# Value rows of even and of odd chunks both whole from DRAM

## The chip, the cores and the metric

The kernel runs on one core of a Trainium2 chip. Five engines work side by side, each through its own list of instructions in order: TensorE (PE, with its weight loads PEld), VectorE (DVE), ScalarE (ACT), GpSimd (POOL) and SyncE (SP). SyncE computes nothing here; it issues every transfer between DRAM and the core's SBUF (128 partitions), and 16 DMA engines carry them out. The metric is the device time of one execution in microseconds (us).

## What is computed

Chunked local attention, then a soft mixture of experts, all in float32. The attention has 4 batches x 8 heads, 768 positions, head size 64. The positions are cut into chunks of 32; each chunk attends to 8 memory rows, the 16 positions before it, its own 32 and the 8 after it, 64 keys in all:

```python
for c in range(nc):
    l_start, r_end = max(0, c_start - 16), min(S, c_end + 8)
    k_full = np.concatenate([mem_k, k[:, :, l_start:r_end]], axis=2)
    v_full = np.concatenate([mem_v, v[:, :, l_start:r_end]], axis=2)
    a = softmax(scale * q_c @ k_full^T)
    out[:, :, c_start:c_end] = a @ v_full
```

Its output x (3072 tokens x 512) goes through the experts: logits x @ phi (32 slots); a softmax over all tokens gives each slot's input; 8 experts with two layers (512 to 1024 to 512, ReLU) work on 4 slots each; a softmax over the slots mixes their outputs back to every token. The expert weights w1 and w2 are 16.8 MB each.

## The kernel before, in words

The attention runs over 12 units of 256 positions (8 chunks, 8 heads). A unit's queries `q_t`, keys `k_t` and values `v_t` lie in one of three buffers each (`NB`), heads in pairs: on the partitions of `k_t` and `v_t` rows of the first and of the second head of a pair alternate, and each has its own half of the free axis, with zeros where the other head's rows are. Those zeros are written once, ahead of the loop; that is why every load of keys or values goes to every second partition, once for each head (`load_k`, `load_v`).

Two neighbouring chunks, an even and an odd one, share 32 of their 64 key rows. Before the change `v_t[i]` is a pair of tiles. The even one takes all 64 rows from the DRAM tensor `vw`, on partitions 0 to 127 in steps of two, 256 KB a head. The odd one takes the 32 rows that it does not share from `vx`, on partitions 0 to 63 in steps of two, 128 KB a head; its partitions 64 to 127 are the even tile's, copied by GpSimd (`share_v`, L150).

The loop over units (L407) interleaves: values of unit i and their normalizing, scores and softmax of unit i + 2, transposes of unit i + 1, and, every second unit, the logits of a group of two units. In each pass SyncE gets, in program order, the values of unit i + 3 (once unit i has used the buffer), weight pieces of 512 KB by a table (`load_w`, 1.5 pieces a pass at first), and keys and queries of unit i + 5. GpSimd gets the key copies `first_k(i + 3)` and `share_v(i + 2)`. After the loop the weights fill what buffers come free, including those of keys, queries, values and x; the experts follow, and `combine` writes the output.

Transfers are carried out in the order of their issue, with at most eight on the way: each has one of eight semaphores, and the ninth waits for the first.

Each engine keeps the order in which the program is written (`InOrder`), so the opening (L188 to L217) fixes what stands behind what: the clears of `k_t` and `v_t` on DVE, ACT and POOL, the loads of units 0 to 2, and the copies of GpSimd between them.

In the row names a tile's buffer number is left out, and a helper records every operation, so that all of them carry the line L65.

Of the kernel before, what the change touches and what calls it, by code (L numbers as in the profile page):

```python
# [10 lines left out]
F32 = mybir.dt.float32  # L11
# [4 lines left out]
P = 128  # L16
B, H, S, D = 4, 8, 768, 64
# [17 lines left out]
NSLOT = 32  # L35
# [35 lines left out]
def tile_attn_softmoe(  # L71
# [2 lines left out]
    qT: bass.AP,  # L74
    kT: list,
    vw: bass.AP,
    vx: bass.AP,
    phi: bass.AP,
    w1: bass.AP,
    w2: bass.AP,  # L80
# [7 lines left out]

    q_t = [cp.tile([P, NPAIR, U], F32, tag=f"q{i}", name=f"q{i}") for i in range(NB)]
    k_t = [cp.tile([P, 2, KW], F32, tag=f"k{i}", name=f"k{i}") for i in range(NB)]  # L90
    v_t = [[cp.tile([P, 2, VW], F32, tag=f"v{i}{o}", name=f"v{i}{o}") for o in range(2)] for i in range(NB)]
    x_t = [cp.tile([P, 4, DM], F32, tag=f"x{i}", name=f"x{i}") for i in range(2)]
    w_slab = [cp.tile([P, PIECE], F32, tag=f"w{i}", name=f"w{i}") for i in range(NW)]
    lT = cp.tile([P, NG, P], F32, tag="lT", name="lT")
    late = [v_t[(NU - NB) % NB][o].rearrange("p a n -> p (a n)") for o in range(2)]
    hT = late[0].rearrange("p (e f s) -> p e f s", e=E, s=NSLOT)
    c_sb = late[1][:, 0:4 * NG * NSLOT].rearrange("p (u s) -> p u s", s=NSLOT)
    cst = [late[1][:, 4 * NG * NSLOT + P * G:4 * NG * NSLOT + P * G + P] for G in range(NG)]
# [16 lines left out]
    def load_q(u):  # L115
        sp.dma_start(q_t[u % NB], qT[u])
# [10 lines left out]
    def load_k(u):  # L127
        for h in range(2):
            sp.dma_start(own_k(u)[h:P:2, h], kT[u % UPB][u // UPB, 64 * h:64 * h + 64])
# [11 lines left out]
        pool.tensor_copy(out=kx[:, :, :, lo:CHUNK], in_=own[:, :, :, 0:CHUNK - lo])  # L141

    def load_v(u):
        e, o = v_t[u % NB]
        for h in range(2):
            sp.dma_start(e[h:P:2, h], vw[u, 64 * h:64 * h + 64])
        for h in range(2):
            sp.dma_start(o[h:P // 2:2, h], vx[u, CHUNK * h:CHUNK * h + CHUNK])

    def share_v(u):  # L150
        e, o = v_t[u % NB]
        pool.tensor_copy(out=o[P // 2:P], in_=e[P // 2:P])

    slabs = list(w_slab)
    freed = []
    for d in range(NB):
        u = NU - NB + d
        flat = k_t[u % NB].rearrange("p a n -> p (a n)")
        freed += [(2 * u - 3, flat[:, 0:PIECE]), (2 * u - 3, flat[:, PIECE:2 * PIECE])]
        freed += [(2 * u - 3, q_t[u % NB].rearrange("p g n -> p (g n)"))]  # L160
        if d:
            freed += [(2 * u, v_t[u % NB][o][:, a]) for o in range(2) for a in range(2)]
    flat_x = [t.rearrange("p u n -> p (u n)") for t in x_t]
    last = (NG - 1) % 2
    freed += [(2 * NU, flat_x[1 - last][:, 0:PIECE]), (2 * NU, flat_x[1 - last][:, PIECE:2 * PIECE])]
# [19 lines left out]

    dve.memset(k_t[0][:, 0], 0.0)  # L188
    dve.memset(warm, 0.0)
    pool.memset(k_t[0][:, 1], 0.0)  # L190
    make_identity(nc, ident)
    load_q(0)
    load_k(0)
    dve.memset(v_t[0][1][0:P // 2], 0.0)
    dve.memset(k_t[1][:, 0], 0.0)
    pool.memset(k_t[1][:, 1], 0.0)
    for u in range(NB):
        e = v_t[u][0].rearrange("p h n -> p (h n)")
        act.copy(out=e, in_=warm[:, 0:1].broadcast_to([P, 2 * VW]))
    load_k(1)  # L200
    load_q(1)
    load_v(0)
    first_k(0)
    dve.memset(v_t[1][1][0:P // 2], 0.0)
    share_v(0)
    load_v(1)
    sp.dma_start(phi_sb, phi.rearrange("(kc p) s -> p kc s", p=P))
    first_k(1)
    dve.memset(k_t[2][:, 0], 0.0)
    pool.memset(k_t[2][:, 1], 0.0)  # L210
    load_k(2)
    load_q(2)
    share_v(1)
    pool.memset(v_t[2][1][0:P // 2], 0.0)
    load_v(2)
    first_k(2)
    load_w(W0)  # L217
# [42 lines left out]
    def softmax(u, tiles):  # L260
        mx = wk.tile([P, 16, 1], F32, tag="mx", name=f"mx{u}")
        p = pexp[u] = wk.tile([P, 8, 4 * CHUNK], F32, tag="p", name=f"p{u}")
        step = NSUB // len(tiles)
        for a, t in enumerate(tiles):
            if u % UPB == 0 and a == 0:
                dve.memset(t[0:32, 0, :, :, 0:LEFT], NEG)
            if u % UPB == UPB - 1 and a == len(tiles) - 1:
                dve.memset(t[96:128, step - 1, :, :, CHUNK - RIGHT:CHUNK], NEG)
            m = mx[:, 8 * step * a:8 * step * (a + 1)]
            dve.tensor_reduce(out=m[:, :, 0], in_=t.rearrange("p s g h n -> p (s g h) n"), axis=AX.X, op=ALU.max)  # L270
            for h in range(2):
                dve.tensor_tensor(
                    out=p[:, 4 * step * a:4 * step * (a + 1)].rearrange("p m (n h) -> p h m n", h=2)[:, h],
                    in0=t.rearrange("p s g h n -> p h (s g) n")[:, h],
                    in1=m.rearrange("p (m h) o -> p h m o", h=2)[:, h].broadcast_to([P, 4 * step, 2 * CHUNK]),
                    op=ALU.subtract,
                )

# [25 lines left out]
    def values(u, pt):  # L304
        a_ps = banks(f"a{u}", "A").rearrange("p s (g h d) -> p s g h d", g=NPAIR, h=2)
        for s in range(NSUB):
            for g in range(NPAIR):
                for j in range(4):
                    v = v_t[u % NB][j % 2].rearrange("p h (i g d) -> p h i g d", g=NPAIR, d=D)
                    pe.matmul(  # L310
                        a_ps[32 * j:32 * j + 32, s, g],
                        lhsT=pt[s][:, g, 32 * j:32 * j + 32],
                        rhs=v[:, :, 2 * s + j // 2, g, :],
                        start=True, stop=True,
                    )
        return a_ps
# [90 lines left out]
    for i in range(NU):  # L407
        G = (i - 2) // 2 if i >= 2 else None
        first = i % 2 == 0
        if i >= 1:  # L410
            transpose_x(i - 1)
        if i + 1 < NU:
            exponent(i + 1)
        if G is not None and not first:
            dispatch_t(G)
        a_ps = values(i, pt)
        if G is not None and first:
            l_ps = logits(G)
        if G is not None and not first:
            dispatch(G)  # L420
        normalize(i, a_ps)
        if i + 3 < NU:
            load_v(i + 3)
        load_w(W0 + int(WRATE * (i + 0.5)) if i < WLAST else usable[2 * i])
        if G is not None and first:
            dispatch_max(G, l_ps)
            dispatch_exp(G, l_ps)
        if G is not None and not first:
            dispatch_z(G)
            dispatch_sum(G)  # L430
        if i + 2 < NU:
            softmax(i + 2, scores(i + 2))
        if i + 1 < NU:
            pt = transpose_p(i + 1)
            normalizer(i + 1)
        if i + 3 < NU:
            first_k(i + 3)
        if i + 2 < NU:
            share_v(i + 2)
        if i + 5 < NU:  # L440
            load_k(i + 5)
            load_q(i + 5)
        load_w(W0 + int(WRATE * (i + 1)) if i < WLAST else usable[2 * i + 1])
        if i == NU - NB + 1:
            pool.memset(hT, 0.0)
# [169 lines left out]
def _layouts(inputs):  # L615
    q, k, v = inputs["q"], inputs["k"], inputs["v"]
    qT = q.reshape(B, NPAIR, 2, UPB, U, D).transpose(0, 3, 5, 2, 1, 4).reshape(NU, P, NPAIR, U)

    def stream(x, mem):
        half = CHUNK // 2  # L620
        parts = [np.zeros((B, H, LEFT, D), x.dtype), x[:, :, :half]]
        for t in range(half, S, 2 * CHUNK):
            parts += [mem, x[:, :, t:t + 2 * CHUNK]]
        parts.append(np.zeros((B, H, RIGHT, D), x.dtype))
        return np.concatenate(parts, axis=2)

    ks = stream(k, inputs["mem_k"]).reshape(B, NPAIR, 2, STREAM, D)
    kT = {}
    for u in range(UPB):
        base = CP * STEP * u  # L630
        chain = [base + STEP * i + r for i in range(CP) for r in list(range(CHUNK)) + list(range(2 * CHUNK, STEP))]
        chain += [base + STEP * CP + r for r in range(HALO)]
        chain = chain[LEFT if u == 0 else HALO:len(chain) - (RIGHT if u == UPB - 1 else 0)]
        both = [base + STEP * i + CHUNK + r for i in range(CP) for r in range(CHUNK)]
        cols = ks[:, :, :, np.array(chain + both)]
        kT[f"k{u}"] = cols.transpose(0, 2, 4, 1, 3).reshape(B, P, NPAIR * NCOL[u])

    vs = stream(v, inputs["mem_v"]).reshape(B, NPAIR, 2, STREAM, D)

    def windows(first):  # L640
        rows = np.array([[[STEP * (CP * u + i) + r for i in range(CP)] for u in range(UPB)] for r in first])
        w = vs[:, :, :, rows]
        return w.transpose(0, 4, 2, 3, 5, 1, 6).reshape(NU, 2 * len(first), CP, NPAIR * D)

    vw = windows(range(2 * CHUNK))
    vx = windows(range(2 * CHUNK, STEP + HALO))
    w2 = inputs["moe_w2"].reshape(E, NFC, P, NBLK, WB).transpose(3, 0, 2, 1, 4).reshape(NBLK, E, P, 2, PIECE)
    return {"qT": qT, **kT, "vw": vw, "vx": vx, "phi": inputs["moe_phi"], "w1": inputs["moe_w1"], "w2": w2}


# [17 lines left out]
```

## Time and profile before

| | |
|---|---|
| runs | 193.74, 190.03, 191.42 us; median 191.42 |
| the profiled execution | 187.95 us, span 186.2 us |
| PE busy | 146.5 us (79%) |
| DVE busy | 101.2 us (54%) |
| ACT busy | 62.7 us (34%) |
| POOL busy | 36.3 us (19%), 22.7 of it copies of values |
| DMA | 63.12 MB, mean 339 GB/s, queue of SyncE 95.2% of 16 engines' span |

Busy time is the time in which an engine ran an instruction; shares are of the span, from the first instruction to the last. The profiled execution's own time is 1.75 us longer than its span, and below the three runs. The DMA share is the mean over 16 DMA engines of the time in which a packet was on the way, so a share of 1.00 says that the engines had work, not that they moved it fast: that is in GB/s.

### The profile page before, as it was taken

The page shows a single profiled execution, that of the slowest core. Times are in us where ns is not written, and L with a number is a line of the kernel's source. Part 1 is how long each engine was busy: PE and PEld are TensorE (multiplying, and loading weights), DVE is VectorE, ACT ScalarE, POOL GpSimd, SP SyncE. Part 2 cuts the span into 40 slices and gives each one's busy share as a digit, 9 for nine tenths or more (in the row PEclk, how much of TensorE's full clock was granted, in tenths as well). Part 3 has the DMA queues.
Part 4 walks back from the last instruction along what each step waited for, and adds up shares of the span by engine and source line. Part 5 has one row for each costly group of instructions (what it writes and reads, how often), then busy time and mean ns, then how long its engine had stood idle before and what let it go on. Part 6 is the DMA issues. An engine that isn't in the chain of part 4 may idle for free.

```text
span 186.2 us, 6128 instructions
## 1 busy us (share of the span) xinstructions
PE 146.5 (79%) x2649; PEld 108.2 (58%) x2649; DVE 101.2 (54%) x179; ACT 62.7 (34%) x122; POOL 36.3 (19%) x43
## 2 busy tenths in 40 slices
PE   4821996884999599789799588579999978867960
PEld 4711795773879488659778485264565635411530
DVE  6860399592679959597899934320560007100360
ACT  7620136231624806354273362200322006000350
POOL 6006901452223404050521800000000000000000
PEclk9996699999699999999999969957999999975576
DMA  5699789999999999999999999999999999999596
GB/s 164 217 276 219 229 258 383 340 392 284 386 293 314 323 338 383 260 362 258 334 303 263 388 402 415 410 407 408 408 410 406 409 406 408 408 411 420 213 407 249
DMA packets 18219, 63.12 MB, mean 339 GB/s; under 512 B 3088, under 2 KB 3088, under 8 KB 18192
## 3 DMA queue, kind: packets, MB, share of 16 engines
q1 hardware_dynamic: 18192, 62.73, 95.2%
q8 instruction: 21, 0.34, 0.8%
q14 instruction: 6, 0.05, 0.1%
HBM read 56.43 MB, written 6.29 MB: 337 GB/s over the span
## 4 chain that ended last, share of the span: by engine, by line
PE 46%; DMA 20%; DVE 16%; issue 7%; ACT 5%; SPq 1%; DVEq 0%; POOL 0%; ACTq 0%
PE s L65 10%; PE a L65 8%; PE h L65 7%; DMA w<-in_w_dram 5%; DMA k<-in_w_dram 5%; DMA v<-in_w_dram 5%; PE xt_ps L65 5%; PE pt_ps L65 4%; DMA v<-in_vw_dram 4%; DVE p L65 4%; DVE z L65 3%; DVE mx L65 3%; PE o L65 3%; ACT v L65 3%; DVE x L65 3%
## 5 line engine op out<-in xcount | busy, mean ns | idle before, releaser
L65 PE MATMUL s<-k,q 128*32 128x128 f32 x768 | 27.5, 292 | 13.9 <-POOL k L65 8.1
L65 PEld LDWEIGHTS s<-k,q 128*32 128x32 f32 x768 | 23.9, 118 | 18.3 <-issue 8.9
L65 POOL COPY v<-v 64x2048 f32<-64x2048 f32 x12 | 22.7, 1896 | 52.0 <-DMA v<-in_vw_dram 37.0
L65 PE MATMUL a<-v,pt 128*32 128x128 f32 x768 | 25.1, 277 | 4.6 <-issue 4.4
L65 ACT COPY pt<-pt_ps 128x512 f32<-128x512 f32 x24 | 13.1, 590 | 40.3 <-PE pt_ps L65 40.1
L65 PEld LDWEIGHTS a<-v,pt 128*32 128x32 f32 x768 | 20.8, 111 | 8.1 <-issue 6.4
L65 DVE TENSOR_REDUCE mx<-s 128x16 f32<-128x1024 f32 (+1 forms) x13 | 14.8, 1142 | 14.0 <-PE s L65 13.7
L65 DVE TENSOR_TENSOR x<-a,z 128x1024 f32<-128x1024 f32 x12 | 14.7, 1224 | 8.1 <-PE a L65 7.2
L65 PE MATMUL pt_ps<-ident,p 128*128 128x128 f32 x96 | 14.6, 298 | 2.5 <-issue 2.3
L65 DVE TENSOR_TENSOR p<-s,mx 128x512 f32<-128x512 f32 (+1 forms) x26 | 15.8, 656 | 0.5
L65 ACT ACTIVATE p<-p 128x1024 f32<-128x1024 f32 (+1 forms) x13 | 12.9, 994 | 7.0 <-DVE p L65 6.7
L65 PE MATMUL xt_ps<-ident,x 128*128 128x128 f32 x96 | 14.5, 298 | 0.9 <-DVE x L65 0.5
L65 ACT COPY xT<-xt_ps 128x512 f32<-128x512 f32 x24 | 13.4, 604 | 4.7 <-PE xt_ps L65 4.7
L65 DVE TENSOR_REDUCE z<-p 128x16 f32<-128x1024 f32 x12 | 14.6, 1214 | 0.0
L65 PEld LDWEIGHTS pt_ps<-ident,p 128*128 128x128 f32 x96 | 11.3, 150 | 5.2 <-issue 4.6
L65 PEld LDWEIGHTS xt_ps<-ident,x 128*128 128x128 f32 x96 | 12.4, 155 | 2.0 <-DVE x L65 1.4
L65 DVE COPY so_sb<-so 128x256 f32<-128x256 f32 x2 | 0.8, 424 | 19.7 <-PE so L65 19.7
L65 PE MATMUL o<-shl,v 32*128 32x256 f32 x96 | 9.8, 530 | 1.4 <-ACT shl L65 0.9
L65 PEld LDWEIGHTS o<-shl,v 32*128 32x128 f32 x96 | 6.5, 249 | 5.0 <-ACT shl L65 2.0
L65 POOL COPY k<-k 128x192 f32<-128x192 f32 (+2 forms) x20 | 5.8, 295 | 17.9 <-DMA k<-in_k_dram 17.2
L65 ACT COPY shl<-r 128x256 f32<-128x256 f32 x2 | 0.7, 373 | 23.5 <-PE r L65 23.5
L65 PE MATMUL h<-w,siT 128*32 128x256 f32 x120 | 8.5, 443 | 0.0
(95 smaller groups left out, 169.9 us busy)
## 6 DMA issues: line engine op xcount, KB each, us to landing
w<-in_w_dram SPq DMA_DIRECT2D x30, 512.0 KB, 9.8
q<-in_qT_dram SPq DMA_DIRECT2D x12, 512.0 KB, 7.2
v<-in_vw_dram SPq DMA_DIRECT2D x24, 256.0 KB, 7.9
k<-in_w_dram SPq DMA_DIRECT2D x12, 512.0 KB, 10.1
v<-in_w_dram SPq DMA_DIRECT2D x12, 512.0 KB, 10.2
v<-in_vx_dram SPq DMA_DIRECT2D x24, 128.0 KB, 7.6
q<-in_w_dram SPq DMA_DIRECT2D x6, 512.0 KB, 10.1
k<-in_k_dram SPq DMA_DIRECT2D x8, 296.0 KB, 7.0
```

What stands on the lines that cost most here:

```text
L65: return self.tc.keep_in_program_order(f(*args, **kwargs))
```

## The change

`v_t[i]` becomes one tile with an axis for even and odd. For each head, one transfer of 512 KB brings both whole: 64 partitions in steps of two, and on each two pieces of 4 KB. `vx` and `share_v` go. To let even and odd chunks use one layout, the rows of a window are ordered so that its two halves alternate (`even`, `odd` in `_layouts`), and the subtraction of the maximum (in `softmax`) writes the scores in that order: it reads PSUM with an innermost axis of two elements, 32 elements apart. phi is laid out by the host so that each partition reads one row of 512 bytes. The opening is written in another order: all four clears of value buffers 0 and 1 on ScalarE, those of buffer 2 on VectorE and GpSimd, the clears of all three key buffers first on VectorE and ahead of the first key copy on GpSimd.

```diff
-    v_t = [[cp.tile([P, 2, VW], F32, tag=f"v{i}{o}", name=f"v{i}{o}") for o in range(2)] for i in range(NB)]
+    v_t = [cp.tile([P, 2, 2, VW], F32, tag=f"v{i}", name=f"v{i}") for i in range(NB)]
...
     def load_v(u):
-        e, o = v_t[u % NB]
+
         for h in range(2):
-            sp.dma_start(e[h:P:2, h], vw[u, 64 * h:64 * h + 64])
-        for h in range(2):
-            sp.dma_start(o[h:P // 2:2, h], vx[u, CHUNK * h:CHUNK * h + CHUNK])
-
-    def share_v(u):
-        e, o = v_t[u % NB]
-        pool.tensor_copy(out=o[P // 2:P], in_=e[P // 2:P])
+            sp.dma_start(v_t[u % NB][h:P:2, :, h], vw[u, 64 * h:64 * h + 64])
...
+    def clear_v(eng, u, o):
+        t = v_t[u][:, o].rearrange("p h n -> p (h n)")
+        if eng is act:
+            act.copy(out=t, in_=warm[:, 0:1].broadcast_to([P, 2 * VW]))
+        else:
+            eng.memset(t, 0.0)
+
+    dve.memset(warm, 0.0)
     dve.memset(k_t[0][:, 0], 0.0)
-    dve.memset(warm, 0.0)
     pool.memset(k_t[0][:, 1], 0.0)
+    for u in range(2):
+        clear_v(act, u, 0)
+        clear_v(act, u, 1)
     make_identity(nc, ident)
+    dve.memset(k_t[1][:, 0], 0.0)
+    pool.memset(k_t[1][:, 1], 0.0)
     load_q(0)
     load_k(0)
-    dve.memset(v_t[0][1][0:P // 2], 0.0)
-    dve.memset(k_t[1][:, 0], 0.0)
-    pool.memset(k_t[1][:, 1], 0.0)
-    for u in range(NB):
-        e = v_t[u][0].rearrange("p h n -> p (h n)")
-        act.copy(out=e, in_=warm[:, 0:1].broadcast_to([P, 2 * VW]))
     load_k(1)
     load_q(1)
-    load_v(0)
-    first_k(0)
-    dve.memset(v_t[1][1][0:P // 2], 0.0)
-    share_v(0)
-    load_v(1)
-    sp.dma_start(phi_sb, phi.rearrange("(kc p) s -> p kc s", p=P))
-    first_k(1)
     dve.memset(k_t[2][:, 0], 0.0)
     pool.memset(k_t[2][:, 1], 0.0)
+    clear_v(dve, 2, 0)
+    first_k(0)
+    load_v(0)
+    load_v(1)
+    sp.dma_start(phi_sb, phi)
+    first_k(1)
+    clear_v(pool, 2, 1)
     load_k(2)
     load_q(2)
-    share_v(1)
-    pool.memset(v_t[2][1][0:P // 2], 0.0)
     load_v(2)
     first_k(2)
...
                 dve.tensor_tensor(
-                    out=p[:, 4 * step * a:4 * step * (a + 1)].rearrange("p m (n h) -> p h m n", h=2)[:, h],
-                    in0=t.rearrange("p s g h n -> p h (s g) n")[:, h],
-                    in1=m.rearrange("p (m h) o -> p h m o", h=2)[:, h].broadcast_to([P, 4 * step, 2 * CHUNK]),
+                    out=p[:, 4 * step * a:4 * step * (a + 1)].rearrange("p m (j s h) -> p h m j s", s=2, h=2)[:, h],
+                    in0=t.rearrange("p s g h (b j) -> p h (s g) j b", b=2)[:, h],
+                    in1=m.rearrange("p (m h) o -> p h m o", h=2)[:, h].rearrange(
+                        "p m (o z) -> p m o z", z=1).broadcast_to([P, 4 * step, CHUNK, 2]),
                     op=ALU.subtract,
                 )
...
-        if i + 2 < NU:
-            share_v(i + 2)
...
-    vw = windows(range(2 * CHUNK))
-    vx = windows(range(2 * CHUNK, STEP + HALO))
+    even = [CHUNK * (r % 2) + r // 2 for r in range(2 * CHUNK)]
+    odd = [CHUNK * (2 - r % 2) + r // 2 for r in range(2 * CHUNK)]
+    vw = np.stack([windows(even), windows(odd)], axis=2)
+    phi = inputs["moe_phi"].reshape(NKC, P, NSLOT).transpose(1, 0, 2)
```

How instructions move, at two places. First GpSimd in the opening; `k_67`, `k_68` and `k_69` are the key buffers 0, 1 and 2, `v_70` and `v_71` the even and odd value tile of buffer 0, `v_72` and `v_73` those of buffer 1. Before:

```order
L65 MEMSET k_68 128x1312
L65 COPY k_67<-k_67 128x2x4x16
L65 COPY v_71<-v_70 64x2048
L65 COPY k_68<-k_67 128x2x4x24
L65 COPY k_68<-k_68 128x2x4x8
L65 MEMSET k_69 128x1312
L65 COPY v_73<-v_72 64x2048
L65 MEMSET v_75 64x2048
```

Now, where `v_72` is the whole value tile of buffer 2:

```order
L65 MEMSET k_68 128x1312
L65 MEMSET k_69 128x1312
L65 COPY k_67<-k_67 128x2x4x16
L65 COPY k_68<-k_67 128x2x4x24
L65 COPY k_68<-k_68 128x2x4x8
L65 MEMSET v_72 128x2048
L65 COPY k_69<-k_68 128x2x4x24
```

The copies of values are gone from between the key copies, and the clear of key buffer 2 stands ahead of all copies.

Second SyncE, from the values of unit 3 to those of unit 4. Before (`v_70` even, `v_71` odd tile of buffer 0, `v_72` and `v_73` of buffer 1, `w_79` and `w_80` weight pieces):

```order
L65 DMA v_70<-in_vw_dram 64x1024 x2
L65 DMA v_71<-in_vx_dram 32x1024 x2
L65 DMA k_69<-in_k_dram 64x1120 x2
L65 DMA q_66<-in_qT_dram 128x1024
L65 DMA w_79<-in_w_dram 128x1024
L65 DMA v_72<-in_vw_dram 64x1024 x2
L65 DMA v_73<-in_vx_dram 32x1024 x2
```

Now (`v_70` and `v_71` are the value tiles of buffers 0 and 1):

```order
L65 DMA v_70<-in_vw_dram 64x2x1024 x2
L65 DMA k_69<-in_k_dram 64x1120 x2
L65 DMA q_66<-in_qT_dram 128x1024
L65 DMA w_76<-in_w_dram 128x1024
L65 DMA v_71<-in_vw_dram 64x2x1024 x2
```

Four transfers of values a unit become two larger ones; the order is otherwise kept.

## Rows read from the trace of the kernel before

**Rows 1.** Page, part 2: tenths and GB/s in 40 slices of 4.65 us.
```profile
PEclk9996699999699999999999969957999999975576
DMA  5699789999999999999999999999999999999596
GB/s 164 217 276 219 229 258 383 340 392 284 386 293 314 323 338 383 260 362 258 334 303 263 388 402 415 410 407 408 408 410 406 409 406 408 408 411 420 213 407 249
```

**Rows 2.** Page, part 4: the chain that ended last, by line.
```profile
PE s L65 10%; PE a L65 8%; PE h L65 7%; DMA w<-in_w_dram 5%; DMA k<-in_w_dram 5%; DMA v<-in_w_dram 5%; PE xt_ps L65 5%; PE pt_ps L65 4%; DMA v<-in_vw_dram 4%; DVE p L65 4%; DVE z L65 3%; DVE mx L65 3%; PE o L65 3%; ACT v L65 3%; DVE x L65 3%
```

**Rows 3.** The chain in order of time: start, us, what.
```profile
33.28 1.96 PE s L65 x64
...
91.20 1.76 PE s L65 x64
...
111.07 1.96 PE a L65 x64
...
160.40 9.99 DMA v<-in_w_dram
...
170.44 1.12 PE so L65 x8
```

**Rows 4.** Windows: stretch, length, each engine's busy us (count), PEclk, DMA share, GB/s.
```profile
0.00:12.50 12.50, 7.42 (x86) 6.61 (x86) 10.05 (x13) 7.41 (x5) 3.26 (x9) 1.00 0.68 215
0.00:30.00 30.00, 19.22 (x344) 17.19 (x346) 18.13 (x26) 12.23 (x13) 11.02 (x17) 0.89 0.81 234
0.00:35.00 35.00, 22.12 (x430) 19.55 (x430) 21.14 (x30) 13.29 (x14) 13.80 (x21) 0.90 0.84 261
30.00:35.00 5.00, 2.90 (x96) 2.36 (x86) 3.01 (x5) 1.06 (x1) 2.78 (x4) 1.00 1.02 419
35.00:37.00 2.00, 2.00 (x27) 1.73 (x16) 1.58 (x3) 1.09 (x3) 0.00 (x0) 1.00 1.07 249
...
95.00:98.00 3.00, 2.98 (x84) 2.11 (x85) 2.97 (x3) 1.81 (x4) 1.35 (x1) 1.00 0.99 358
98.00:101.50 3.50, 3.49 (x78) 3.02 (x67) 3.24 (x7) 0.74 (x2) 0.54 (x1) 1.00 0.97 233
30.00:101.50 71.50, 60.77 (x1426) 52.04 (x1417) 55.31 (x86) 29.81 (x58) 21.50 (x24) 0.98 1.00 325
104.00:170.00 66.00, 55.50 (x761) 32.09 (x753) 20.64 (x56) 15.09 (x39) 2.80 (x2) 0.89 1.03 408
```

**Rows 5.** Page, part 6: issues, KB each, median us to landing.
```profile
v<-in_vw_dram SPq DMA_DIRECT2D x24, 256.0 KB, 7.9
...
v<-in_vx_dram SPq DMA_DIRECT2D x24, 128.0 KB, 7.6
```

**Rows 6.** Timeline of SyncE: start, us until the last issue, what, count.
```profile
28.61 1.82 SPq L65 DMA_DIRECT2D v<-in_vw_dram  x2
31.13 1.14 SPq L65 DMA_DIRECT2D v<-in_vx_dram  x2
```

**Rows 7.** Timeline of GpSimd in the opening; in brackets idle time before, and its end.
```profile
15.43 1.89 POOL L65 COPY v<-v 64x2048 f32<-64x2048 f32 x1 [8.60 <-DMA v<-in_vw_dram]
17.39 0.52 POOL L65 COPY k<-k 128x192 f32<-128x192 f32 x2
```

**Rows 8.** Timeline of TensorE in the opening: the scores of unit 1.
```profile
17.96 3.64 PE L65 MATMUL s<-k,q 128*32 128x128 f32 x64 [7.44 <-POOL k L65]
```

**Rows 9.** Lines of VectorE by form: shapes, count | busy us, mean ns | idle before.
```profile
L65 DVE TENSOR_TENSOR p<-s,mx 128x512 f32<-128x512 f32 x22 | 14.3, 699 | 0.4
...
L65 DVE TENSOR_SCALAR z<-z 128x16 f32<-128x16 f32 x12 | 5.8, 483 | 0.4
...
L65 DVE TENSOR_REDUCE stats<-l 128x1 f32<-128x128 f32 x6 | 1.7, 283 | 2.2 <-PE l L65 2.2
...
L65 DVE TENSOR_SCALAR cz<-cz 128x12 f32<-128x12 f32 x2 | 0.3, 174 | 0.1
L65 DVE TENSOR_REDUCE nms<-nm_ps 32x32 f32<-32x128 f32 x1 | 0.3, 278 | 1.0 <-PE nm_ps L65 1.0
```

More of the change, by code (lines that the diff above doesn't have):

```diff
@@ L76, in tile_attn_softmoe @@
     vw: bass.AP,
-    vx: bass.AP,
     phi: bass.AP,
@@ L94, in tile_attn_softmoe @@
     lT = cp.tile([P, NG, P], F32, tag="lT", name="lT")
-    late = [v_t[(NU - NB) % NB][o].rearrange("p a n -> p (a n)") for o in range(2)]
+    late = [v_t[(NU - NB) % NB][:, o].rearrange("p a n -> p (a n)") for o in range(2)]
     hT = late[0].rearrange("p (e f s) -> p e f s", e=E, s=NSLOT)
@@ L160, in tile_attn_softmoe @@
         freed += [(2 * u - 3, q_t[u % NB].rearrange("p g n -> p (g n)"))]
-        if d:
-            freed += [(2 * u, v_t[u % NB][o][:, a]) for o in range(2) for a in range(2)]
+    for u in range(NU - NB + 1, NU):
+        freed += [(2 * u, v_t[u % NB][:, o, a]) for o in range(2) for a in range(2)]
     flat_x = [t.rearrange("p u n -> p (u n)") for t in x_t]
@@ L308, in values @@
                 for j in range(4):
-                    v = v_t[u % NB][j % 2].rearrange("p h (i g d) -> p h i g d", g=NPAIR, d=D)
+                    v = v_t[u % NB][:, j % 2].rearrange("p h (i g d) -> p h i g d", g=NPAIR, d=D)
                     pe.matmul(
@@ L421, in tile_attn_softmoe @@
         normalize(i, a_ps)
-        if i + 3 < NU:
-            load_v(i + 3)
+        if i + NB < NU:
+            load_v(i + NB)
         load_w(W0 + int(WRATE * (i + 0.5)) if i < WLAST else usable[2 * i])
@@ L643, in windows @@
         return w.transpose(0, 4, 2, 3, 5, 1, 6).reshape(NU, 2 * len(first), CP, NPAIR * D)
-    vw = windows(range(2 * CHUNK))
-    vx = windows(range(2 * CHUNK, STEP + HALO))
+    even = [CHUNK * (r % 2) + r // 2 for r in range(2 * CHUNK)]
+    odd = [CHUNK * (2 - r % 2) + r // 2 for r in range(2 * CHUNK)]
+    vw = np.stack([windows(even), windows(odd)], axis=2)
+    phi = inputs["moe_phi"].reshape(NKC, P, NSLOT).transpose(1, 0, 2)
     w2 = inputs["moe_w2"].reshape(E, NFC, P, NBLK, WB).transpose(3, 0, 2, 1, 4).reshape(NBLK, E, P, 2, PIECE)
-    return {"qT": qT, **kT, "vw": vw, "vx": vx, "phi": inputs["moe_phi"], "w1": inputs["moe_w1"], "w2": w2}
+    return {"qT": qT, **kT, "vw": vw, "phi": phi, "w1": inputs["moe_w1"], "w2": w2}
 def kernel(**inputs):
```

## The prediction

> **What bounds the kernel now.** I read the busy slices first. From the fourth slice to the end of the thirty-eighth the 16 DMA engines are busy nearly all the time, while the rate under them is uneven: 219 to 392 GB/s in the attention stage, 401 to 420 GB/s once only weights move [rows 1]. So transfers set the pace, and in the attention stage they are slow transfers. The chain of waits says the same of the end: the last weight pieces follow each other, ten microseconds each from issue to landing, and TensorE takes the last of them at 170.44 [rows 3]. Whatever shortens or lengthens the queue of transfers ahead of that piece moves the end; behind it lie 15.8 us to the end of the span (186.2) that the change does not touch.
>
> Then I looked at the queue by stretches. Between 30.0 and 101.5 us it moves at 325 GB/s with a share of 1.00, against 408 GB/s for weights alone [rows 4]. That mean hides two speeds: fast stretches (419 GB/s in 30 to 35, 358 in 95 to 98) and slow ones (249 in 35 to 37, 233 in 98 to 101.5); there are nine of each, and the slow ones last 2.0 to 4.3 us [rows 4]. What lies in a slow stretch follows from the order of the queue. By 35.0 us 261 GB/s x 35 = 9.1 MB have moved [rows 4]. Summed in the order of issue, queries and keys of units 0 to 4, values of units 0 to 2, phi, one weight piece and the two `vw` transfers of unit 3 are 9.06 MB. So the fast stretch 30 to 35 holds keys of unit 4, its queries and the even value rows of unit 3, and the slow one begins just where the two `vx` transfers of unit 3 come up; SyncE had issued them next after `vw` [rows 6]. There are nine `vx` pairs after the opening and nine slow stretches. `vw` and keys are also stored on every second partition, but over all 128; `vx` goes to partitions 0 to 63 only. I take this place to be the cause.
>
> [...]
>
> **The change, part by part.**
>
> *Bytes.* A unit's values were 2 x 256 and 2 x 128 KB [rows 5]; now they are 2 x 512 KB. That is 0.262 MB more a unit, 3.1 MB in all.
>
> *The steady stretch, 30 to 101.5.* It moved 325 x 71.5 = 23.2 MB and holds nine value sets; now 25.6 MB. How fast a transfer of 64 partitions with two 4 KB pieces each goes, no row shows. Bounds: the weights' 408 GB/s give 62.7 us (8.8 less than 71.5); today's mean of 325 gives 78.8 us (7.3 more). The nearest row is 30 to 35, half of it strided stores over all partitions, at 419; but 358 occurs too, so I take 385: 66.5 us, **5.0 us less**.
>
> *The opening, queue.* 7.0 MB had moved by 30.0 and 2.7 MB by 12.5 [rows 4]: 247 GB/s between. The same place in the queue now lies at 7.8 MB. From 12.5 on 5.1 MB remain: 13.3 us at 385 (25.8, or 4.2 less), 20.7 us at 247 (33.2, or 3.2 more). The order on SyncE also frees the keys of units 1 and 2 from waits for buffer clearing (three of DVE's clears now stand in a row, POOL's third clear no longer stands behind a value copy); I put 1 us on that, between 0 and 2. **5 us less.**
>
> [...]
>
> *GpSimd's copies in the loop.* Twelve of 1.9 us go. They lie beside other work, except that VectorE's small scaling of z takes 483 ns in the mean while one of like kind takes 174 [rows 9]: 12 x 0.31 = 3.7 us on VectorE, at most, come back. I count 0 for the end, where the queue binds.
>
> *The subtraction on VectorE* now reads PSUM with a stride of 32 elements. The row with such a read (nms, 128 elements in columns of stride 32) took 278 ns, the plain one of 128 elements (stats) 283 [rows 9]: I take 0. The other bound is a doubling, 0.7 us on each of 22. [...]
>
> *phi as one row a partition, two transfers less a unit on SyncE, the clears of value tiles moved to ScalarE and VectorE*: 64 KB in larger pieces, issue time beside a queue that is 7.6 to 7.9 us deep [rows 5], and work ahead of the first scores. Nothing, unless ScalarE's fourth clear is late for unit 1's values; they queue behind unit 0's anyhow.
>
> *Sum.* 5.0 + 5 = 10 us. The profiled execution took 187.95 us (span 186.2), so 178. It lies below all runs shown (190.03 to 193.74, median 191.42), 3.5 us under their median: **181.5 us**, 5% less.
>
> **Rivals.**
>
> *Strided stores are slow as such.* [...] For it: no row shows this transfer, and slow stretches also hold keys. Against it: 30 to 35 holds strided stores at 419. It decides from 340 GB/s down: there 25.6 MB take 75.3 us, 3.8 more, which the opening (15.1 us for 5.1 MB, 2.4 less, and 1 of order) just gives back. Chance 0.13.
>
> *Compute becomes the bound.* The scores of units 3 and 10 start at 33.28 and 91.20 [rows 3]: 8.27 us a unit. The queue now takes 71.5 / 9 = 7.9 and would take 7.4. [...] Against it: VectorE's 3.7 us come back, and about 8 us of lead have to be used up first. Chance 0.14.
>
> *The strided PSUM read is slow.* `DVE p` holds 4% of the chain [rows 2]; doubled, 6.5 us more: 188 us. Chance 0.06.
>
> *Nothing comes of it*: faster transfers only meet later waits (weight buffers that TensorE frees, at values of the last unit at 111.07 [rows 3]): 188 to 192 us. Chance 0.07.
>
> **How the numbers follow.** The forecast has 0.60. Its own range: 408 GB/s in both stretches and 2 us of order give 8.8 + 5.0 + 2 = 15.8, so 176; 350 GB/s gives 25.6 MB in 73.1 (1.6 more) and 14.6 in the opening (2.9 less), so 189 with 1 us of order. With the second, third and fourth rival inside, 174.5 to 192 leaves out the first rival and little at the low end. About 2% (3.8 us, so 187.6 and 195.2) can be told from no change: faster 0.76 (the forecast but for its slowest end, most of the second rival, a little of the third), the same 0.13, slower 0.11.
>
> **What would show it.** In the profile after: slow stretches of 230 to 270 GB/s gone between 25 and 95 us, the rate there 370 or more; the second scores at 11 to 13.5 instead of 17.96, with a granted clock near 1.0 there; the subtraction still 700 ns; the small scaling of z near 175 ns; the last weight piece taken by TensorE near 160. It would be wrong if the new value transfers run at 340 GB/s or less, if TensorE waits for values in the loop, or if the queue's share falls clearly under 1.0 there.

## The result and the profile after

The changed kernel takes 177.96 us in the median (176.39 to 178.41, four runs), the kernel before 190.72 (188.99 to 193.74, four runs beside them): a ratio of 0.934, 95% interval 0.924 to 0.945. By the ratio it is 6.6% faster, where 5% was forecast. Executions more than 1.5% above the fastest of the same kernel are left out of the ratios here and below, while medians and ranges are those of all executions. The profiled executions took 176.39 us with a span of 174.6, against 187.95 and 186.2.

The page of the changed kernel, part 2: the granted clock in tenths, the DMA engines' share and their rate in 40 slices, here of 4.37 us each.

```profile
PEclk9999999996999999999999999965999999999995
DMA  4899999999999999999999999999999999999993
GB/s 146 289 340 412 419 417 414 405 407 416 406 410 413 405 395 393 394 324 341 354 330 410 413 412 406 410 407 289 353 413 417 407 410 406 409 407 419 414 417 130
```

The alternation of fast and slow slices of before [rows 1] is gone: from the fourth slice on most stand at 405 to 419. Two shallow places are left, slices 18 to 21 and slices 28 and 29. The windows of the same execution (stretch, length, busy us of each engine, granted clock, DMA share, GB/s) give the places that the prediction speaks of.

```profile
0.00:12.50 12.50, 9.31 (x94) 8.11 (x98) 8.39 (x12) 9.51 (x7) 6.94 (x14) 1.00 0.75 252
0.00:23.70 23.70, 18.02 (x302) 15.65 (x302) 15.51 (x24) 12.97 (x13) 7.21 (x15) 1.00 0.88 329
23.70:89.60 65.90, 57.23 (x1374) 49.99 (x1372) 49.67 (x80) 29.84 (x59) 4.06 (x15) 0.97 1.01 389
30.00:67.00 37.00, 32.01 (x742) 27.92 (x743) 26.90 (x43) 16.65 (x32) 2.18 (x8) 0.95 1.02 407
75.00:90.00 15.00, 14.66 (x370) 12.52 (x365) 13.43 (x23) 8.09 (x16) 0.29 (x2) 1.00 0.98 331
...
118.00:126.00 8.00, 8.00 (x111) 4.09 (x107) 2.07 (x5) 1.21 (x2) 0.00 (x0) 0.77 0.93 317
```

329 GB/s x 23.7 us = 7.8 MB: the place in the queue that the forecast put at 25.8 us, less 1 for SyncE's order, is reached at 23.7. The 25.6 MB behind it take 65.9 us. TensorE's scores in the opening (timeline; units 0, 1, 2):

```profile
6.98 3.64 PE L65 MATMUL s<-k,q 128*32 128x128 f32 x64 [2.14 <-POOL k L65]
...
12.12 2.10 PE L65 MATMUL s<-k,q 128*32 128x128 f32 x64
...
20.06 1.95 PE L65 MATMUL s<-k,q 128*32 128x128 f32 x64 [2.14 <-DVE x L65]
```

Unit 1's start at 12.12 instead of 17.96 and take 2.10 us instead of 3.64 [rows 8], at a granted clock of 1.00 (first two windows). VectorE by form, the rows that answer to [rows 9]:

```profile
L65 DVE TENSOR_TENSOR p<-s,mx 128x512 f32<-128x512 f32 x22 | 14.3, 696 | 0.4
...
L65 DVE TENSOR_SCALAR z<-z 128x16 f32<-128x16 f32 x12 | 2.1, 175 | 0.4
```

And the chain of waits in order of time (start, us, what):

```profile
84.19 1.75 PE s L65 x62
...
102.69 1.96 PE a L65 x64
...
116.55 6.15 PE h L65 x64
...
147.72 0.39 PE o L65
148.11 10.12 DMA v<-in_w_dram
158.23 0.04 issue
158.28 0.68 PE so L65 x8
```

The last piece is taken at 158.28 instead of 170.44 [rows 3]. What is new is what stands ahead of it: TensorE's own work back to the attention, with one transfer at the very end, where before several transfers of weights stood in a row.

### The profile page after: what moved, and what is told of

Same layout as the page of the kernel before. It is cut to its first block, busy times and chain, and to the rows that moved or that the text cites. A ratio compares the mean times of both kernels' runs of the same rounds, so it can differ in the third digit from the quotient of the medians.

```text
span 174.6 us, 6046 instructions
## 1 busy us (share of the span) xinstructions
PE 140.3 (80%) x2649; PEld 106.0 (61%) x2649; DVE 95.6 (55%) x178; ACT 63.7 (36%) x123; POOL 13.1 (7%) x31
## 4 chain that ended last, share of the span: by engine, by line
PE 63%; DVE 12%; issue 8%; DMA 8%; ACT 3%; POOL 1%; DVEq 0%; ACTq 0%; POOLq 0%
PE s L65 14%; PE a L65 11%; PE h L65 10%; DMA v<-in_w_dram 6%; PE xt_ps L65 5%; PE pt_ps L65 5%; PE so L65 4%; PE D_ps L65 3%; PE l L65 3%; DVE x L65 2%; PE o L65 2%; DVE p L65 2%; DVE mx L65 2%; DMA k<-in_k_dram 2%; DVE z L65 2%
## 5 line engine op out<-in xcount | busy, mean ns | idle before, releaser
L65 PEld LDWEIGHTS s<-k,q 128*32 128x32 f32 x768 | 23.4, 115 | 15.4 <-issue 9.8
L65 PE MATMUL a<-v,pt 128*32 128x128 f32 x768 | 25.8, 277 | 3.0 <-issue 2.6
L65 PE MATMUL xt_ps<-ident,x 128*128 128x128 f32 x96 | 13.6, 286 | 0.7 <-DVE x L65 0.5
L65 PE MATMUL pt_ps<-ident,p 128*128 128x128 f32 x96 | 13.5, 283 | 0.6 <-issue 0.6
L65 PEld LDWEIGHTS xt_ps<-ident,x 128*128 128x128 f32 x96 | 11.6, 148 | 2.5 <-DVE x L65 1.4
L65 PEld LDWEIGHTS pt_ps<-ident,p 128*128 128x128 f32 x96 | 10.4, 142 | 2.4 <-issue 2.2
L65 PE MATMUL h<-w,siT 128*32 128x256 f32 x120 | 9.4, 484 | 0.0
L65 PE MATMUL o<-shl,v 32*128 32x256 f32 x96 | 7.7, 409 | 1.9 <-ACT shl L65 0.9
L65 ACT ACTIVATE hs<-h,rzd 128x512 f32<-128x512 f32 x4 | 2.8, 689 | 17.2 <-PE h L65 17.2
L65 PE MATMUL l<-xT,phi_sb 128*32 128x128 f32 x192 | 7.9, 274 | 0.8 <-issue 0.7
L65 DVE MEMSET s<- 32x128 f32 (+1 forms) x8 | 1.1, 138 | 13.2 <-PE s L65 13.2
```

The lines of the kernel that those rows point to most:

```text
L65: return self.tc.keep_in_program_order(f(*args, **kwargs))
```

## The experiments

The theory was that a transfer onto one half of the partitions is slow, and that the changed kernel gains because no transfer of values does that any more. Its rivals were the number or size of the transfers, GpSimd's copies, and the order of the opening. Ratios are against runs of the kernel before, taken beside them.

**Values cut at partition 64.** The changed kernel, each head's transfer in two, one to each half:

```diff
-            sp.dma_start(v_t[u % NB][h:P:2, :, h], vw[u, 64 * h:64 * h + 64])
+            for m in range(2):
+                lo = 64 * m + h
+                sp.dma_start(v_t[u % NB][lo:64 * m + 64:2, :, h], vw[u, 64 * h + 32 * m:64 * h + 32 * m + 32])
```

> The changed kernel with each head's 512 KB of values cut at partition 64: one transfer of 256 KB to every second partition of 0 to 63, one to those of 64 to 127; same bytes, four transfers a unit instead of two. Theory of the halves (a transfer onto one half of the partitions is slow): before, 0.262 MB a unit of that kind cost (71.5 - 23.2 / 0.408) / 9 = 1.6 us a unit more than at the weights' rate. Now it is 1.05 MB a unit: at least twice its time at 408 GB/s, 2.6 us more a unit, 31 us in all, so 209 us; 6.4 us more a unit and 255 us if the cost of before grows with the bytes. Rival, the number of transfers (four small ones a unit were slow, wherever they go): 1.6 us a unit comes back, 178 + 12 x 1.6 = 197 us. Rival, the size of 128 KB: pieces of 256 KB are fast, 178 us.

Measured: 215.86 us (209.13 to 219.86), ratio 1.121 (1.100 to 1.142). Its steady stretch, in which SyncE issues the values of units 3 to 11:

```profile
30.00:120.00 90.00, 64.22 (x1455) 54.56 (x1447) 53.68 (x87) 31.08 (x60) 5.86 (x16) 0.96 1.03 278
```

25.0 MB in 90.0 us, which at the changed kernel's 389 GB/s would take 64.3: 25.7 us more. If the stretch holds the values of units in the changed kernel's proportion, these are 25.0 / 25.6 x 9 = 8.8 units, and it is 2.9 us a unit. The 1.05 MB of a unit take 2.6 us at 408 GB/s, so here 5.5, which is 191 GB/s: an estimate, and about half the rate. The theory's lower end (twice the time) holds; both rivals fall.

**Values cut into fourths.** The control: as many transfers of the same size, but each over all partitions.

```diff
-            sp.dma_start(v_t[u % NB][h:P:2, :, h], vw[u, 64 * h:64 * h + 64])
+            for m in range(2):
+                lo = 2 * m + h
+                sp.dma_start(v_t[u % NB][lo:P:4, :, h], vw[u, 64 * h + m:64 * h + 64:2])
```

> The changed kernel with each head's 512 KB of values cut into two transfers of 256 KB that each go to every fourth partition of all 128: as many transfers and bytes as in the run with halves, other partitions. Theory of the halves: each reaches both halves, so nothing changes, 176 to 180 us, and 380 GB/s or more between 25 and 90 us. Rival, the number of transfers: 197 us, as for the halves. Rival, the spacing (the wider the partitions of a transfer lie apart, the slower): slower than 181 us, with stretches under 300 GB/s.

Measured: 178.94 us (176.63 to 180.62), ratio 0.945 (0.929 to 0.961), the changed kernel's within the interval.

```profile
25.00:90.00 65.00, 56.71 (x1360) 49.55 (x1362) 50.13 (x81) 29.88 (x59) 4.05 (x15) 0.97 1.00 391
```

The rate is 391 GB/s. Which partitions a transfer reaches makes 33 us between these two kernels, by their ratios (1.121 - 0.945, of 189 us); how many transfers there are, and how far apart their partitions lie, makes nothing that shows.

**The kernel before with `vx` spread.** This edit, with the odd tiles cleared whole ahead of the loop:

```diff
-            sp.dma_start(o[h:P // 2:2, h], vx[u, CHUNK * h:CHUNK * h + CHUNK])
+            sp.dma_start(o[h:P:4, h], vx[u, CHUNK * h:CHUNK * h + CHUNK])
```

> The kernel before with one edit: the vx transfers of 128 KB go to every fourth partition of all 128 instead of every second of 0 to 63 (the odd chunks' values then stand in wrong rows, and their buffers are cleared whole). Bytes, number and size of transfers and GpSimd's copies stay. Theory of the halves: the nine slow stretches vanish, 385 to 410 GB/s between 30 us and the end of the attention's loads; there 23.2 MB take 57 to 60 us instead of 71.5, but the attention's compute, 8.2 us a unit, keeps part of it, so 180 to 185 us. Rivals, the number of transfers, their size, or GpSimd's copies: 189 to 192 us, slow stretches as before.

Measured: 182.59 us (180.24 to 183.73), ratio 0.963 (0.948 to 0.979).

```profile
30.00:60.00 30.00, 24.96 (x594) 21.83 (x593) 20.93 (x30) 10.91 (x19) 12.24 (x15) 0.94 1.01 393
30.00:93.00 63.00, 54.87 (x1278) 46.75 (x1280) 51.05 (x77) 27.01 (x54) 21.26 (x24) 0.97 0.99 361
```

30 to 60 us runs at 393 GB/s (344 in the kernel before) with every copy still there, so the cause is in `vx`'s partitions. Over the whole stretch it is 361, not the 385 to 410 expected: 333 GB/s from 60 us on, where the share is 0.96. The time came out as forecast; the rate in the second half did not.

**The kernel before without the copies.** `share_v` does nothing, and the odd tiles are cleared whole:

```diff
-        pool.tensor_copy(out=o[P // 2:P], in_=e[P // 2:P])
+        pass
```

> The kernel before without GpSimd's twelve copies of the shared value rows (the upper half of the odd tiles keeps its zeros, so this part of the values is left out). The transfers are as before. Theory of the halves: the slow stretches of 230 to 270 GB/s stay and the rate between 30 and 101.5 stays near 325; only the second scores come sooner (13 instead of 17.96 us) and the small scaling of z falls to 175 ns, off the path: 187 to 191 us. Rival, the copies hold up the transfers or the compute: 180 to 185 us, slow stretches gone.

Measured: 189.17 us (185.50 to 192.56), ratio 0.999 (0.989 to 1.009).

```profile
30.00:101.50 71.50, 59.98 (x1460) 51.66 (x1452) 53.46 (x88) 30.44 (x61) 5.28 (x14) 1.00 1.00 314
```

```profile
L65 DVE TENSOR_SCALAR z<-z 128x16 f32<-128x16 f32 x12 | 2.2, 181 | 0.4
```

```profile
12.86 1.95 PE L65 MATMUL s<-k,q 128*32 128x128 f32 x64 [1.32 <-DMA q<-in_qT_dram]
...
24.46 3.54 PE L65 MATMUL s<-k,q 128*32 128x128 f32 x64 [3.50 <-DMA q<-in_qT_dram]
```

It is the copies that make the scaling of z slow in the mean (181 ns without them) and hold the second scores back (12.86 without them). But the third scores then wait for queries, start at 24.46 (25.05 in the profile of before), and the end does not move. 314 GB/s: the slow transfers are not the copies' doing.

**`vx` on the upper half.** The kernel before mirrored:

```diff
-            sp.dma_start(o[h:P // 2:2, h], vx[u, CHUNK * h:CHUNK * h + CHUNK])
+            sp.dma_start(o[P // 2 + h:P:2, h], vx[u, CHUNK * h:CHUNK * h + CHUNK])
...
-        pool.tensor_copy(out=o[P // 2:P], in_=e[P // 2:P])
+        pool.tensor_copy(out=o[0:P // 2], in_=e[0:P // 2])
```

> The kernel before mirrored: vx goes to every second partition of 64 to 127 and GpSimd copies the lower half (the odd chunks' values then stand in wrong rows). Theory of the halves: the upper half is as slow as the lower, 325 GB/s in the steady stretch and 188 to 192 us. Rival, partitions 0 to 63 alone are slow (something else lies there, or is stored there at the time): 180 to 185 us, as when the vx transfers were spread.

Measured: 192.13 us (188.45 to 197.45), ratio 1.004 (0.997 to 1.012).

```profile
30.00:101.50 71.50, 52.74 (x1242) 45.55 (x1234) 48.80 (x76) 25.38 (x49) 19.13 (x23) 0.96 1.01 300
```

Either half is slow: with `vx` on the upper one the time is not told from that on the lower one (1.004). The rate, 300 GB/s where 325 was expected, is that of the longest of the ten executions (197.45 us), so it does not say that the upper half is the slower one.

**One head on each half.** `vx` of the first head below, of the second above:

```diff
-            sp.dma_start(o[h:P // 2:2, h], vx[u, CHUNK * h:CHUNK * h + CHUNK])
+            sp.dma_start(o[(P // 2) * h + h:(P // 2) * (h + 1):2, h], vx[u, CHUNK * h:CHUNK * h + CHUNK])
```

> The kernel before with vx of the first head on every second partition of 0 to 63, as it is, and of the second head on every second of 64 to 127 (the odd chunks' values then stand in wrong rows; their buffers are cleared whole). If a transfer is slow by its own half, whatever its neighbours in the queue do: 188 to 192 us and 325 GB/s in the steady stretch, as before. If neighbours overlap, so that what counts is the half that a stretch of the queue goes to (in the changed kernel cut in halves, in which the halves alternated, 1.05 MB cost some 3 us a unit more, in the kernel before 0.262 MB on one half 1.6 us): 183 to 187 us, and 345 to 380 GB/s.

Measured: 188.16 us (185.50 to 190.08), ratio 0.990 (0.976 to 1.003).

```profile
30.00:101.50 71.50, 59.25 (x1434) 50.33 (x1427) 57.20 (x87) 29.07 (x58) 21.32 (x24) 0.99 1.02 339
```

This is inconclusive: the time is that of the first theory (188 to 192 us), and the rate (339) lies between the two (325, and 345 to 380).

**The opening in its old order.** The changed kernel with these lines in the order of before; the core of the edit:

```diff
-    for u in range(2):
-        clear_v(act, u, 0)
-        clear_v(act, u, 1)
...
+    clear_v(dve, 0, 1)
     dve.memset(k_t[1][:, 0], 0.0)
     pool.memset(k_t[1][:, 1], 0.0)
-    load_q(0)
-    load_k(0)
+    for u in range(NB):
+        clear_v(act, u, 0)
...
+    clear_v(dve, 1, 1)
     load_v(1)
```

> The changed kernel with the clears, loads and key copies of the opening in the order of before (no value copies among them; the clears of odd value tiles now 128 partitions instead of 64). Theory of the prediction: the order itself is worth about 1 us (0 to 2), the rest of the opening's gain comes from faster value transfers and from the copies that are gone: 178 to 181 us, second scores by 14 us. Rival, the order is most of the opening's gain: 183 to 186 us, second scores after 16 us.

Measured: 178.79 us (178.23 to 184.12), ratio 0.941 (0.935 to 0.947). The second scores start at 12.96. There are 0.8 us between the medians, and the intervals overlap: the order is worth about what was put on it, or nothing.

**Even halves alone.** What sets the end now:

```diff
-            sp.dma_start(v_t[u % NB][h:P:2, :, h], vw[u, 64 * h:64 * h + 64])
+            sp.dma_start(v_t[u % NB][h:P:2, 0, h], vw[u, 64 * h:64 * h + 64, 0])
```

> The changed kernel with the even half of each value transfer alone (the odd chunks' values stay zero, so that part is left out): 6.3 MB less on the queue, 15.4 us at 408 GB/s; all else as it is. Theory that the queue still sets the end: 163 to 166 us. Theory that the attention's compute now sets it, with the weight pieces that no buffer can take before the experts begin (64 pieces, 36 of them into buffers beforehand, so 28 x 0.524 MB / 408 GB/s = 36 us after the experts' start at 116.55, where 41.7 us passed): the end moves by 5.7 us at most, and less where attention is no faster: 172 to 177 us, and the experts start at 114 us or later.

Measured: 174.38 us (171.78 to 176.45 in three executions, and 713.62 in the fourth), ratio 0.905 (0.897 to 0.913).

```profile
25.00:90.00 65.00, 56.40 (x1315) 49.79 (x1304) 47.37 (x78) 28.01 (x55) 3.16 (x12) 0.95 0.86 302
```

```profile
116.09 5.17 PE L65 MATMUL h<-w,siT 128*32 128x256 f32 x64
...
158.41 0.64 PE L65 MATMUL so<-v,v 128*32 128x256 f32 x8 [0.61 <-DMA v<-in_w_dram]
```

6.3 MB less, worth 15.4 us of queue, give 5.6 us by the ratios (0.905 against the changed kernel's 0.934, of 190 us). So the queue still sets the end of the changed kernel, but for some 6 us only: the theory of the queue alone (163 to 166 us) falls, and the other theory's bound (5.7 us at most) holds at its edge. In the attention the queue now stands idle at times (share 0.86). What takes over isn't shown: in the profiled execution the experts start at 116.09 (116.48 for this row in the changed kernel) and the last piece comes as late as there, but it took 176.45 us, 4 more than each of the two shortest.

**Two more weight buffers.** `hs`, `so` and `shl` take over finished tiles of `p` and `xT`, and:

```diff
-NW = 15
+NW = 17
```

> The changed kernel with 17 weight buffers instead of 15, in room that three small tiles of the experts' stage give up (they take the place of tiles of the attention that are done by then). If the end is now set by the attention's compute and, behind the experts' start, by the pieces that no buffer could take before, these are 26 instead of 28: 2 x 0.524 MB / 408 GB/s = 2.6 us less, 175 to 176.5 us. Rival, the queue sets the end: two more pieces can't be moved before the experts start, no change, 177 to 179 us.

Measured: 176.34 us (174.69 to 178.67), ratio 0.934 (0.925 to 0.943).

```profile
118.00:126.00 8.00, 8.00 (x126) 4.49 (x118) 2.81 (x8) 1.90 (x3) 0.00 (x0) 0.94 1.03 408
```

```profile
115.91 5.16 PE L65 MATMUL h<-w,siT 128*32 128x256 f32 x64
...
156.84 0.64 PE L65 MATMUL so<-q,v 128*32 128x256 f32 x8 [0.59 <-DMA q<-in_w_dram]
```

The gap at 118 to 126 (317 GB/s in the changed kernel) closes, and the last piece comes 1.4 us sooner, not 2.6; behind it this kernel takes 174.2 - 156.84 = 17.4 us instead of 16.3. Its ratio can't be told from the changed kernel's. The direction in the profile is the theory's; a gain in time is not shown.

**A version between both.** From unit 3 on the even tile from DRAM, copied whole by GpSimd, and the odd chunks' own rows stored over it, spread over all partitions:

```diff
+    def share_v(u):
+        pool.tensor_copy(out=v_t[u % NB][:, 1], in_=v_t[u % NB][:, 0])
+
+    def load_own(u):
+        for h in range(2):
+            sp.dma_start(v_t[u % NB][h:P:4, 1, h], vw[u, 64 * h:64 * h + 64:2, 1])
...
             first_k(i + 3)
+        if NB <= i + 2 < NU:
+            share_v(i + 2)
...
+        if NB <= i + 2 < NU:
+            load_own(i + 2)
```

> A version between both: from unit 3 on, the even tile comes whole from DRAM as in the changed kernel, GpSimd copies it whole onto the odd tile (128 partitions, 1.9 us), and then the odd chunks' own 32 rows a head are stored over it, 128 KB on every fourth partition of all 128. 9 x 0.262 = 2.36 MB less than the changed kernel, 5.8 us of queue at 408 GB/s. If attention's compute keeps its pace, the end moves by what is in flight when the experts start: 2 to 5 us, so 173 to 176 us. Rival, the new waits (a transfer that waits for GpSimd, with SyncE's later issues behind it) or the slower scaling of z beside GpSimd's copies (483 against 175 ns, 3.7 us in all) cost as much: 177 to 182 us.

Measured: 186.11 us (183.83 to 190.18), ratio 0.973 (0.965 to 0.981): slower than the changed kernel with fewer bytes. Its list of waits, three rows:

```profile
POOL v L65 <- DMA v<-in_vw_dram: 29.1, 6, 7.0
...
PE s L65 <- issue: 11.9, 4, 4.7
...
PE a L65 <- DMA v<-in_vw_dram: 4.5, 3, 3.1
```

The time lies outside both ranges, above the rival's 177 to 182. The rival's mechanism is there: GpSimd waits for the even rows and TensorE, three times, for values, which the changed kernel never does in the loop. TensorE also stood still 4.7 us in the scores of unit 5, released by nothing that the profile shows. These rows are of the longest of the six executions (190.18 us), and what each wait makes of the 7 us between the two kernels (0.973 against 0.934) was not tried.

## Why the prediction was right, point by point

**The slow stretches.** Right, and the cause is shown, not only argued: the transfer's partitions alone, edited in the kernel before, take 3.7% off its time (ratio 0.963), and in the changed one, between fourths and halves, add 33 us. The stretch of 25.6 MB was put at 66.5 us and took 65.9. That 385 and 389 GB/s agree is partly luck: 30 to 67 us run at 407, near the upper bound, and 75 to 90 at 331, with 268 from 78 to 80, inside the 230 to 270 that the prediction wanted gone. No transfer of values onto one half explains that. How slow a transfer onto one half is, the kernel cut in halves shows: 191 GB/s by the estimate, against 408 for weights alone. Either half is so: the run on the upper half has a ratio of 1.004. Why such a transfer is slow, no run shows.

**The opening's queue.** The term was 5 us, and it is 6.3: the place reached at 30.0 before comes at 23.7. By 12.5 us 252 x 12.5 = 3.15 MB had moved instead of 2.7, and the 4.65 MB behind them ran at 415 GB/s instead of the 385 taken. The 1 us for SyncE's order is not refuted (0.8, not told from 0).

That the term came out near its size is partly luck, since what it was added up from did not hold. The prediction put 4.2 us on faster transfers and 1 on the waits for clears. Before, SyncE stood still for 5.4 us in three waits until GpSimd was done with a key buffer (total, times, longest), against 2.1 us in five waits now; GpSimd's clear of key buffer 2 lay behind its copy of unit 0's values:

```profile
SPq L65 <- POOL k L65: 5.4, 3, 3.1
```

The first 30 us with `vx` spread and the copies kept, and without the copies and `vx` as it was:

```profile
0.00:30.00 30.00, 19.21 (x345) 16.97 (x346) 18.69 (x27) 12.58 (x14) 11.02 (x17) 0.83 0.73 241
...
0.00:30.00 30.00, 19.31 (x310) 16.80 (x314) 17.62 (x25) 11.49 (x12) 7.77 (x17) 0.89 0.87 271
```

The 7.0 MB that before had moved by 30.0 have moved by 29.5 with spread transfers alone, while the queue stands idle at times (share 0.73), and by 26.9 with the copies alone gone. With both gone, in the run with the old order, the same place in the queue (7.8 MB) is reached at 24.8, and in the changed kernel at 23.7. So the waits behind the copies, put at 1 us, are worth 3.1 by themselves, and the faster transfers, put at 4.2, 0.5; the rest comes only when both are gone. phi's new layout, which the run with the old order has too, is not told apart in it.

**The opening's compute.** Right: 12.12, clock 1.00. The run without copies shows that GpSimd's copy of unit 0's values, with the key copies behind it [rows 7], had held the second scores (12.86 without it, and 1.95 us instead of 3.64 [rows 8]), and also that this alone moves nothing: its steady stretch runs at 314 GB/s, and the lead is lost there. The run with `vx` spread moves the experts' start to 122.16 from 124.86. Both together, in the run with the old order, have the fourth scores at 28.25 instead of 33.28, 5.0 us sooner and more than the two apart (31.59 and 32.57, 1.7 and 0.7 us sooner): copies and slow transfers each hid part of the other.

**The loop's copies, the subtraction, phi.** Right: the scaling of z takes 175 ns, 3.7 us less in all as put down, and the subtraction 696 against 699, so the strided read cost nothing and the rival of the strided read falls. phi and the moved clears were not tried apart.

**The sum.** 10 us were forecast. The last piece came 12.2 us sooner, the span is 11.6 shorter, since 0.5 us more lie behind that piece. The terms give 6.3 + 5.6 = 11.9: the opening was sized 1.3 too small, the steady stretch (71.5 - 65.9) 0.6. The median was put at 181.5, 3.5 above what was measured, within the forecast's own range of 176 to 189: 2.8 of that are gain that was not forecast (12.8 between the medians, not 10), and 0.7 come from the kernel before, whose median is now 190.72 and not 191.42.

**Which rivals.** Strided stores are not slow as such; that run is the one with fourths, at 391 GB/s where this rival, put at 201 us, kept the 325 of before. The rival of compute is the point where the prediction's picture was too simple. It was given 0.14 and 184.8 us, on 6.7 us of gain for the attention, by which alone the end would move. The 6.7 us were the author's estimate for the second scores, 5 us sooner and 1.7 shorter. There the runs agree (5.1 and 1.7 without the copies, 5.8 and 1.5 in the changed kernel), but no run shows that the attention gains just that. The attention gained 8.4 (experts at 116.48 instead of 124.86), of which 6.3 already at the scores of unit 3 (26.94 instead of 33.28), but the last piece came 12.2 sooner, so the end did not move only as the attention does. The run with even halves shows another bound near by: of 15.4 us taken out of the queue 5.6 reach the end. That this bound is the attention's compute, with the weight pieces that no buffer can take before the experts start, is the theory of that run and not shown.

## What to carry to other kernels

Read the rate of the DMA engines beside their share: a full share at a rate that swings between two levels asks which transfers lie in the slow stretches and which partitions they reach, and spreading them can be worth more bytes (here a share of 1.00 at 325 GB/s, where weights alone had 408, and 3.1 MB more with a ratio of 0.934). When two waits hide each other, removing one shows little until the other is gone too (unit 3's scores came 1.7 us sooner without the copies, 0.7 with spread transfers, 5.0 with both, phi's layout included), so cost such edits together. And when one bound has moved by 10 us, price the next by taking bytes out of it before saving more of them.

## What the runs showed of the hardware that was not expected

- What the 0.262 MB of `vx` a unit cost depends on the rate that they are held against: (71.5 - 23.2 / 0.389) / 9 = 1.3 us at the changed kernel's rate, 0.8 us at the 361 GB/s of the run with `vx` spread, where half the rate would cost 0.64; 1.05 MB in halves cost 2.9, near 2.6. So it is not shown that a small transfer onto one half costs more for its size than a large one. Whether neighbours in the queue pay for it was tried (one head on each half) and stays open.
- 331 GB/s at a share of 0.98 in 75 to 90 us of the changed kernel, while no transfer goes to one half. From 60 to 93 us the kernels without such transfers are all slower than from 30 to 60: 365 against 409 GB/s in the changed kernel, 366 against 408 with fourths, 333 against 393 with `vx` spread. The kernel before has 321 against 344, so a part of its slow rate there may not be `vx`'s. The cause is open.
- VectorE's scaling of 16 columns is not slowed in proportion by GpSimd's copies: in four cases it ended with the copy. Of the twelve in the kernel before, eight take 0.17 or 0.18 us; the four that begin 0.6 us or more before a copy of values ends take 0.64, 0.77, 1.12 and 1.87 us and end 0.03 to 0.04 us after that copy. The mean of 483 ns (and one of 603 in the version between both) says how often the two met. The first such pair, scaling and copy:

```profile
39.27 0.64 DVE L65 TENSOR_SCALAR z<-z 128x16 f32<-128x16 f32 x1
37.98 1.89 POOL L65 COPY v<-v 64x2048 f32<-64x2048 f32 x1 [3.16 <-DMA v<-in_vw_dram]
```
